# Reordering the first batch of an attention and feed-forward kernel: half of q behind w3, a turn on TensorE, loads without a gate

## The chip, the cores and the metric

The kernel runs on one core of one Trainium2 chip. The metric is the time of one execution on the device in microseconds (us). Three executions of the kernel before gave 397.36, 397.40 and 397.75; the median is 397.4.

The engines of the core work in parallel and meet through semaphores: PE (TensorE, matrix products, with PEld for its weight loads), DVE (VectorE), ACT (ScalarE), POOL (GpSimd, which here mostly issues loads and stores) and SP (SyncE, which here issues the crossbar transposes). PSUM has eight banks, into which PE writes; DVE and ACT read them.

## The reference

A Linformer attention feeds a feed-forward network with a maximum of three products. Batch 8, 8 heads, sequence 1024, head size 64; 64 projected keys; model width 512, inner width 768. All is float32 outside the kernel.

```python
k_proj = einsum('ks,bhsd->bhkd', E, k)
v_proj = einsum('ks,bhsd->bhkd', F, v)
scores = matmul(q, k_proj^T) / sqrt(64)
attn   = softmax(scores)                  # over the 64 projected keys
x      = matmul(attn, v_proj)             # heads side by side: [8192, 512]
h      = maximum(maximum(x @ w1, x @ w2), x @ w3)
out    = h @ w_out                        # [8192, 512]
```

## The kernel before

The kernel works in bfloat16 with sums in float32. The loads convert the type on the way. A batch has two chunks of 512 rows; the feed-forward of a chunk is 18 steps of four 128x512 products (`l1`: six column groups, each with w1, w2 and w3) and four down steps of six products. The attention of the next batch is laid between these steps. The first chunk is special: its weights are still arriving, so it goes through w1, then w2, then w3, and starts on the first half of a weight when that half is there.

The loads at the start, in the order in which POOL issues them (k, v and w1 of the first batch come before):

```python
for wt, w in zip(w_sb[1:], (w2, w3)):
    for hh in range(2):
        if wt is w_sb[2] and hh:
            nc.gpsimd.dma_start(out=q_1, in_=qv_[1])        # q of batch 0, chunk 1
        nc.gpsimd.dma_start(out=wt[:, 2*hh:2*hh+2, :], in_=w[hh*256:(hh+1)*256]...)
...                                                         # cut: work on chunk 0
for x in range(2):
    nc.gpsimd.dma_start(out=wo_sb[:, 3*x:3*x+3], in_=w_out...)
load(1, k, k_t); load(1, v, v_t); load(1, q, q_t)           # batch 1
```

The projection of a batch, its turn, and the gate of the loads after it:

```python
def kv(b, bank=AB):
    for si in range(SI):                                    # eight steps
        nc.tensor.matmul(out=ps[0:KP, bank, :], lhsT=eT[:, si, :], rhs=k_t[i][:, :, si, :], ...)
        nc.tensor.matmul(out=ps[KP:P, bank, :], lhsT=fT[:, si, :], rhs=v_t[i][:, :, si, :], ...)
    nc.scalar.copy(out=kp2[i][:, :, :, 0, :], ...)          # k projected, out of PSUM
    nc.scalar.copy(out=vp2[b % 3][KP:P], ...)
    nc.vector.tensor_copy(out=kp_[:, :, 1:], ...)           # k four times side by side
    nc.vector.tensor_copy(out=vp2[b % 3][0:KP], ...)
    nc.sync.dma_start_transpose(out=kpT[i]..., in_=kp2[i]...)   # the crossbar turns it

def load_behind_turn(b, order="qkv", q_of=None):
    nc.gpsimd.tensor_copy(out=seen, in_=kpT[(b - 1) % NB][:, 0, 0, 0:1])   # the gate
    ...                                                     # cut: load q, k, v of batch b
```

The scores of batch 1 (`scores`, line 143 in the profile) multiply `kpT` with `qT`, which DVE's block transposes (`q_flip`, line 103) make from `q_t`.

The first chunk's steps with w2 and w3, and what lies between them (`tick` counts a slot and starts what `at` has set for it):

```python
def l1_first(i, jts, banks, between=None):
    for hh in range(2):
        if hh and between:
            between()
        for jt, bank in zip(jts, banks):
            for ct in (2 * hh, 2 * hh + 1):
                nc.tensor.matmul(out=ps[:, bank, :], lhsT=w_sb[i][:, ct, ...], rhs=xT[0][:, ct, 0, :], ...)
            if hh:
                nc.vector.tensor_tensor(out=h1c[jt] if i == 1 else hT[0][:, jt, :], ..., op=ALU.max)
                yield

if b == 0:
    at(9, scores_up0)            # scores of batch 0, chunk 1: 64 small products, 4 exponentials
    at(12, sums0, 1, 4)          # their sums: 8 products, logarithm, reciprocal
    at(19, kv, 1)
    ...                          # cut: q_flip at 21, 22, 24, 25; gated loads of batch 2 at 22
    at(27, scores, 1, 0); at(30, scores, 1, 1); at(33, sums, 1)
    ...
for part in ((1, range(6), (6, 7, 0, 1, 4, 5)), (2, range(3), (2, 3, 0), q_up0), (2, range(3, 6), (1, 2, 3))):
    for _ in l1_first(*part):
        tick()
for x in range(2):
    if x:
        av_up0()                 # 16 products with v, 4 divisions on DVE (norm0)
    for tt in range(4):
        down_half(tt, x)         # three products each
        if x: tick()
```

`q_up0` is one DVE block transpose of all of `q_1`. Chunk 1 of batch 0 follows: 18 `l1` steps on slots 17 to 34, and then four down steps.

Of the kernel before, what the change touches and what calls it, by code (L numbers as in the profile page):

```python
# [9 lines left out]
FP32 = mybir.dt.float32  # L10
# [6 lines left out]
def kernel(ctx: ExitStack, tc: tile.TileContext, q, k, v, E, F, w1, w2, w3, w_out, out):  # L17
    nc = tc.nc
    B, H, S, D = q.shape
    KP = E.shape[0]  # L20
# [11 lines left out]
    def T(shape, dt, name):  # L32
        return sb.tile(shape, dt, name=name)

    ps = pp.tile([P, 8, 512], FP32, name="ps")
    psb = ps.rearrange("p b n -> p (b n)").bitcast(BF16).rearrange("p (b n) -> p b n", b=8)

    ident = T([P, P], BF16, "ident")
# [9 lines left out]
    NB = 2  # L48
    k_t = [T([P, H, SI, D], BF16, f"k_t{i}") for i in range(NB)]
    v_t = [T([P, H, SI, D], BF16, f"v_t{i}") for i in range(NB)]  # L50
    q_t = [T([P, H, SI, D], BF16, f"q_t{i}") for i in range(NB)]
    qT = [T([P, H, SI * D], BF16, f"qT{i}") for i in range(NB)]
    kp2 = [T([KP, H, 2, 4, D // 2], BF16, f"kp2_{i}") for i in range(NB)]
    kpT = [T([P, H, 2, KP], BF16, f"kpT{i}") for i in range(NB)]
# [18 lines left out]
    q_1 = q_t[0].rearrange("p h si d -> p (h si d)")[:, 4 * H * D:].rearrange("p (h n d) -> p h n d", h=H, d=D)  # L73
# [41 lines left out]
    AB = 4  # L115
    HD = D // 2

    def kv(b, bank=AB):
        i = b % NB
        for si in range(SI):  # L120
            nc.tensor.matmul(out=ps[0:KP, bank, :], lhsT=eT[:, si, :], rhs=k_t[i][:, :, si, :],  # L121
                             start=(si == 0), stop=(si == SI - 1))
            nc.tensor.matmul(out=ps[KP:P, bank, :], lhsT=fT[:, si, :], rhs=v_t[i][:, :, si, :],  # L123
                             start=(si == 0), stop=(si == SI - 1))
        kp_ = kp2[i].rearrange("k h f r dd -> k (h f) r dd")
        kv_v = ps[KP:P, bank, :].rearrange("p (g u dd f) -> p u g f dd", u=2, f=2, dd=HD)
        nc.scalar.copy(out=kp2[i][:, :, :, 0, :], in_=ps[0:KP, bank, :].rearrange("p (h dd f) -> p h f dd", dd=HD, f=2))  # L127
        nc.scalar.copy(out=vp2[b % 3][KP:P], in_=kv_v[:, 1])
        nc.vector.tensor_copy(out=kp_[:, :, 1:], in_=kp_[:, :, 0:1].to_broadcast([KP, 2 * H, 3, HD]))  # L129
        nc.vector.tensor_copy(out=vp2[b % 3][0:KP], in_=kv_v[:, 0])  # L130
        nc.sync.dma_start_transpose(out=kpT[i].rearrange("p h f k -> p (h f) k"),
                                    in_=kp2[i].rearrange("k h f r dd -> k (h f r dd)"))

    def scores(b, u):
        i = b % NB
# [57 lines left out]
    def fbank():  # L193
        ring.append(ring.pop(0))
        return ring[-1]
# [65 lines left out]
    def quads0(ch, bank, lhs, hhs=(0, 1)):  # L261
        for hh, j, g, u in QUADS:
            if hh not in hhs:
                continue
            rows = half(g, u)
            nc.tensor.matmul(out=ps[j * HD:(j + 1) * HD, bank + hh, :], lhsT=lhs(rows, g),  # L266
                             rhs=pT[0][rows, g, ch, :], start=True, stop=True, tile_position=(rows.start, j * HD))
# [24 lines left out]
    def sums0(ch, bank):  # L292
        quads0(ch, bank, lambda rows, g: ones[rows, :])
        nc.scalar.activation(out=lns[ch], in_=ps[:, bank:bank + 2, :], func=AF.Ln)
        nc.scalar.activation(out=rinv[ch], in_=lns[ch], func=AF.Exp, scale=-1.0)
# [7 lines left out]
    def norm0(ch, half, bank, hhs):  # L303
        for hh in hhs:
            nc.vector.tensor_tensor(out=xT[0][:, 2 * hh + half, ch, :], in0=ps[:, bank + hh, :],
                                    in1=rinv[ch][:, hh * 512:(hh + 1) * 512], op=ALU.mult)
# [9 lines left out]

    qT_1 = qT[0][:, 4:8].rearrange("p a n -> p (a n)").rearrange("p (h n) -> p h n", h=H)

    def q_up0():
        nc.vector.transpose(out=qT_1.bitcast(FP32).rearrange("p h n -> p (h n)"),  # L320
                            in_=q_1.rearrange("p h n d -> p (h n d)").bitcast(FP32))

    def scores_up0():
        for g in range(NPAIR):
# [12 lines left out]
    def av_up0():  # L337
        for f, bank in enumerate((6, 4)):
            quads0(1, bank, lambda rows, g: vp2[0][rows, g, f, :])
        norm0(1, 0, 6, (0, 1))  # L340
        norm0(1, 1, 4, (0, 1))

    def warmup(n, bank):
        for _ in range(n):
# [7 lines left out]
    qv_ = q[0].rearrange("h (ch p n) d -> ch p h n d", ch=2, p=P)  # L352
# [18 lines left out]
    for wt, w in zip(w_sb[1:], (w2, w3)):  # L371
        for hh in range(2):
            if wt is w_sb[2] and hh:
                nc.gpsimd.dma_start(out=q_1, in_=qv_[1])
            nc.gpsimd.dma_start(out=wt[:, 2 * hh:2 * hh + 2, :],
                                in_=w[hh * 256:(hh + 1) * 256].rearrange("(r f) n -> r f n", f=2))
    nc.vector.memset(ones, 1.0)

    for u in range(2):
        for f in range(2):  # L380
            nc.vector.tensor_copy(out=sel[:, 2 * u + f, :].rearrange("p (r dd) -> p r dd", r=4),
                                  in_=ident[:, None, u * D + f:(u + 1) * D:2].to_broadcast([P, 4, HD]))
# [106 lines left out]
    for b in range(B):  # L489
        n = b + 1  # L490
        groups = []

        def at(slot, f, *args):
            groups.append((slot, lambda: f(*args)))

        if b == 0:
            at(9, scores_up0)
            at(12, sums0, 1, 4)
            at(19, kv, 1)
            for g, x in enumerate((21, 22, 24, 25)):  # L500
                at(x, q_flip, 1, g)
            at(22, load_behind_turn, 2, "kvq")
            at(27, scores, 1, 0)
            at(30, scores, 1, 1)
            at(33, sums, 1)
            at(33, log, 1)
            at(34, recip, 0)
            at(35, av3, 1)
            at(36, recip, 1)
            at(36, norm, 1, 1, 0, AB)  # L510
            at(38, norm, 1, 0, 1, AB + 2)
        elif b == 1:
            at(2, kv, 2)
            for g in range(4):
                at(4 + g, q_flip, 2, g)
            at(9, load_behind_turn, 3, "kvq")
            at(9, scores, 2, 0)
            at(12, scores, 2, 1)
            at(16, av1, 1)
            at(16, sums, 2)  # L520
            at(16, log, 1)
            at(17, recip, 0)
            at(19, recip, 1)
            at(24, load, 4, k, k_t)
            at(24, load, 4, v, v_t)
            at(25, av3, 2)
            at(26, norm, 2, 1, 0, AB)
            at(28, norm, 2, 0, 1, AB + 2)
            at(30, kv, 3)
            for g in range(4):  # L530
                at(32 + 2 * g, q_flip, 3, g)
        elif n < B:
            if b + 2 < B:
                at(3, lambda: kv(b + 2, fbank()))
            at(3, scores, n, 0)
            at(8, scores, n, 1)
            if b + 3 < B:
                at(11, load_behind_turn, b + 3, "qkv", 4 if b == 2 else None)
            at(14, av1, b)
            at(14, sums, n)  # L540
            at(14, log, 1)
            at(15, recip, 0)
            at(17, recip, 1)
            at(26, av3, n)
            at(27, norm, n, 1, 0, AB)
            at(29, norm, n, 0, 1, AB + 2)
            if b + 2 < B:
                for g in range(4):
                    at(33 + 2 * g, q_flip, b + 2, g)
        else:  # L550
            at(5, av1, b)
        slot = 0
        gi = 0

        def tick():
            nonlocal slot, gi
            slot += 1
            while gi < len(groups) and groups[gi][0] <= slot:
                groups[gi][1]()
                gi += 1  # L560

        for ch in range(2):
            c = 2 * b + ch
            if c == 0:
                for part in ((1, range(6), (6, 7, 0, 1, 4, 5)), (2, range(3), (2, 3, 0), q_up0), (2, range(3, 6), (1, 2, 3))):
                    for _ in l1_first(*part):
                        tick()
                ring[:] = [0, 1, 2, 3]
                for x in range(2):
                    if x:  # L570
                        av_up0()
                    for tt in range(4):
                        down_half(tt, x)
                        if x:
                            tick()
                continue
            for s in range(18):
                l1(b, ch, c, s // 3, s % 3)
                tick()
                if pend and s in (2, 5, 8, 11):  # L580
                    pend.pop(0)()
                    tick()
            pend = [lambda tt=tt, b=b, ch=ch, c=c: down(b, ch, c, tt) for tt in range(4)]
        if b == 0:
            while pend:
                pend.pop(0)()
                tick()
# [32 lines left out]
```

The softmax here doesn't subtract the row's maximum and nothing guards it: scores larger than these inputs give would overflow.

## Time and profile before

| engine or part | busy us or share |
|---|---|
| span of the profiled execution | 395.7 us |
| PE | 383.8 us, 97% |
| DVE | 202.8 us, 51% |
| ACT | 161.8 us, 41% |
| POOL | 66.4 us, 17% |
| POOL's DMA queue, share of 16 engines | 53.1% |
| SP's DMA queue, share of 16 engines | 5.2% |

A page of the profile has, besides busy times, the chain of work that ended last (each piece is followed back to what released it), groups of instructions with what ended the idle time before them, and a timeline. In the timeline a line is a run of like instructions: start and length in us, engine, source line, operation, what is written and read, form and count; a bracket gives the idle time of the engine just before it and what ended it. Matmuls are pipelined, so their recorded lengths overlap. PEldq is the queue of PE's weight loads: its semaphore waits are listed apart. A DMA whose buffer or queue slot is not free holds up POOL, so POOL's idle times tell when earlier transfers landed.

### The profile page before, as it was taken

What the parts mean: (1) busy time and instruction counts of PE and PEld (TensorE: products, weight loads), DVE (VectorE), ACT (ScalarE), POOL (GpSimd) and SP (SyncE); (2) the same over time, 40 slices, a digit from 0 to 9 for tenths busy, and PEclk for the clock granted to TensorE, in tenths of its full rate; (3) what the DMA queues carried; (4) which work ended last, traced back from release to release, by engine and by line L of the source; (5) the groups of instructions that cost most, each with busy time, mean ns of one, the idle gap of its engine ahead of it and who ended that gap; (6) DMA issues with size and microseconds to landing.
All of it is one profiled execution on the core that took longest, in us unless ns stands there. A gap on an engine that the chain in (4) does not pass through costs nothing.

```text
span 395.7 us, 6653 instructions
## 1 busy us (share of the span) xinstructions
PE 383.8 (97%) x2717; PEld 173.4 (44%) x2768; DVE 202.8 (51%) x302; ACT 161.8 (41%) x248; POOL 66.4 (17%) x109
## 2 busy tenths in 40 slices
PE   8999989999999999999999999999999999999996
PEld 4444434444444444444444444444444444444443
DVE  3447475655662476425764347625664356443342
ACT  4413437455326613356224632266234452222221
POOL 7452123062002501050000500000010000000000
PEclk9999999999999999999999999999999999999999
DMA  8999989979963996169711893121011111101023
GB/s 222 206 208 206 206 156 195 242 112 206 206 157 80 170 206 170 42 118 204 180 57 28 152 206 124 53 59 62 15 53 55 53 55 54 55 34 73 0 106 106
DMA packets 41437, 48.39 MB, mean 122 GB/s; under 512 B 9152, under 2 KB 36544, under 8 KB 41408
## 3 DMA queue, kind: packets, MB, share of 16 engines
q0 software_dynamic: 31776, 43.52, 53.1%
q1 hardware_dynamic: 8656, 3.41, 5.2%
q10 hardware_dynamic: 976, 1.05, 0.8%
q8 instruction: 21, 0.34, 0.4%
q14 instruction: 8, 0.07, 0.0%
HBM read 57.15 MB, written 16.78 MB: 187 GB/s over the span
## 4 chain that ended last, share of the span: by engine, by line
PE 88%; DMA 9%; issue 1%; ACT 0%; DVE 0%; POOL 0%; POOLq 0%; DVEq 0%
PE ps L210 57%; PE ps L235 19%; DMA w_sb<-in_moe_w_dram 3%; PE ps L121 3%; PE ps L157 3%; DMA v_t<-in_v_dram 3%; PE ps L143 2%; DMA k_t<-in_k_dram 2%; DMA kpT<-kp 2%; PE ps L248 1%; PE ps L448 1%; PE ps L228 1%; PE ps L123 0%; PE ps L266 0%; DVE hT L217 0%
## 5 line engine op out<-in xcount | busy, mean ns | idle before, releaser
L210 PE MATMUL ps<-xT,w_sb 128*128 128x512 bf16 x1049 | 242.8, 379 | 1.7
L210 PEld LDWEIGHTS <-w_sb 128*128 128x128 bf16 x1080 | 103.6, 98 | 129.9 <-issue 8.4
L215 DVE TENSOR_TENSOR m<-ps,h1s 128x512 f32<-128x512 f32 x90 | 62.1, 690 | 130.8 <-PE ps L210 99.9
L235 PE MATMUL ps<-wo_sb,hT 128*128 128x512 bf16 x335 | 82.3, 379 | 0.5 <-issue 0.2
L213 ACT COPY h1s<-ps 128x512 f32<-128x512 f32 x90 | 52.9, 588 | 68.6 <-PE ps L210 68.2
L237 ACT COPY o_acc<-ps 128x512 f32<-128x512 f32 x58 | 34.0, 586 | 100.9 <-PE ps L235 85.3
L217 DVE TENSOR_TENSOR hT<-ps,m 128x512 bf16<-128x512 f32 x90 | 62.0, 689 | 11.6 <-PE ps L210 3.9
L242 POOL DMA_DIRECT2D out_dram<-o_acc x28 | 15.2, 541 | 262.9 <-ACT o_acc L237 260.4
L235 PEld LDWEIGHTS <-hT 128*128 128x128 bf16 x348 | 33.5, 98 | 41.4 <-issue 1.9
L175 DVE TENSOR_TENSOR xT<-ps,rinv 128x1024 bf16<-128x1024 f32 x28 | 33.5, 1217 | 9.3 <-PE ps L157 7.3
L148 ACT ACTIVATE pT<-ps 128x1024 bf16<-128x1024 f32 x28 | 27.1, 1020 | 7.6 <-PE ps L143 7.3
L103 DVE STREAM_TRANSPOSE qT<-q_t 128x512 f32<-128x512 f32 x28 | 18.6, 689 | 0.0
L89 POOL DMA_DIRECT2D v_t<-in_v_dram x21 | 15.3, 751 | 10.3 <-DMA q_t<-in_q_dram 3.9
L166 ACT ACTIVATE lns<-ps 128x1024 f32<-128x1024 f32 x14 | 13.6, 1020 | 5.5 <-PE ps L157 5.5
L169 ACT ACTIVATE rinv<-lns 128x1024 f32<-128x1024 f32 x14 | 14.8, 1059 | 0.0
L121 PE MATMUL ps<-k_t,eT 128*64 128x512 bf16 x56 | 13.6, 382 | 0.0
L123 PE MATMUL ps<-v_t,fT 128*64 128x512 bf16 x56 | 13.4, 381 | 0.0
L127 ACT CAST kp<-ps 64x512 bf16<-64x512 f32 x7 | 4.0, 578 | 18.8 <-PE ps L123 18.8
L448 PE MATMUL ps<-xT,w_sb 128*128 128x512 bf16 x46 | 10.6, 379 | 1.0 <-DMA w_sb<-in_moe_w_dram 0.8
L89 POOL DMA_DIRECT2D k_t<-in_k_dram x14 | 10.7, 773 | 3.9 <-DMA k_t<-in_k_dram 1.6
L89 POOL DMA_DIRECT2D q_t<-in_q_dram x14 | 10.6, 777 | 2.1 <-DMA wo_sb<-in_moe_w_out_dram 1.1
L129 DVE COPY kp<-kp 64x1536 bf16<-64x1536 bf16 x7 | 3.9, 552 | 13.1 <-ACT kp L127 13.1
(87 smaller groups left out, 162.5 us busy)
## 6 DMA issues: line engine op xcount, KB each, us to landing
out_dram<-o_acc POOLq DMA_DIRECT2D x30, 512.0 KB, 2.9
q_t<-in_q_dram POOLq DMA_DIRECT2D x15, 512.0 KB, 12.1
k_t<-in_k_dram POOLq DMA_DIRECT2D x14, 512.0 KB, 12.4
v_t<-in_v_dram POOLq DMA_DIRECT2D x18, 256.0 KB, 14.7
v_t<-in_v_dram POOLq DMA_DIRECT2D x7, 512.0 KB, 14.4
w_sb<-in_moe_w_dram POOLq DMA_DIRECT2D x4, 384.0 KB, 10.3
k_t<-in_k_dram POOLq DMA_DIRECT2D x4, 256.0 KB, 8.0
w_sb<-in_moe_w_dram POOLq DMA_DIRECT2D x4, 192.0 KB, 10.0
```

The source lines that it names most:

```text
L89: nc.gpsimd.dma_start(out=dst[b % NB][:, slots], in_=sv[:, heads])
L103: nc.vector.transpose(out=qT[b % NB][:, hs].bitcast(FP32).rearrange("p h n -> p (h n)"), in_=q_t[b % NB][:, hs].rearrange("p h si d -> p ( ...
L121: nc.tensor.matmul(out=ps[0:KP, bank, :], lhsT=eT[:, si, :], rhs=k_t[i][:, :, si, :], start=(si == 0), stop=(si == SI - 1))
L148: nc.scalar.activation(out=pT[i][:, 2 * u + gg].rearrange("p ch (t r n) -> p r (ch t) n", t=4, r=4), in_=ps[:, AB:AB + 4, gg * 256:(gg + 1 ...
L175: nc.vector.tensor_tensor(out=xT[b % 2][:, f::2, ch, :], in0=ps[:, bank:bank + 2, :], in1=rinv[ch].rearrange("p (u n) -> p u n", u=2), op= ...
L210: nc.tensor.matmul(out=ps[:, bank, :], lhsT=w_sb[i][:, ct, jt * P:(jt + 1) * P], rhs=xT[b % 2][:, ct, ch, :], start=(ct == 0), stop=(ct == ...
L213: nc.scalar.copy(out=h1s[jt % 2], in_=ps[:, bank, :])
L215: nc.vector.tensor_tensor(out=m12[jt % 2], in0=ps[:, bank, :], in1=h1s[jt % 2], op=ALU.max)
L217: nc.vector.tensor_tensor(out=hT[c % 2][:, jt, :], in0=ps[:, bank, :], in1=m12[jt % 2], op=ALU.max)
L235: nc.tensor.matmul(out=ps[:, bank, :], lhsT=hT[c % 2][:, jt, tt * P:(tt + 1) * P], rhs=wo_sb[:, jt, :], start=(jt == 0), stop=(jt == NJT - 1))
L237: nc.scalar.copy(out=o[:, tt, :], in_=ps[:, bank, :])
L242: nc.gpsimd.dma_start(out=dst[:, tt - 1:tt + 1, :], in_=o[:, tt - 1:tt + 1, :])
```

## The change

The diff rearranges the first batch and touches nothing from batch 1 on. Its aims: let w3's last half arrive before the half of q that is needed later; let the projection of batch 1 start when v is there; take the crossbar, which shares the DMA engines with the loads, out of the way between that projection and the scores; and let batch 2's loads start without waiting for that turn.

```diff
-    def kv(b, bank=AB):
+    def kv(b, bank=AB, crossbar=True):
...
-        nc.sync.dma_start_transpose(...)
+        if crossbar:
+            nc.sync.dma_start_transpose(...)
+
+    def kp_turn(b):
+        i = b % NB
+        for h in range(H):
+            for f in range(2):
+                x = ((h % 4) * 2 + f) * KP
+                nc.tensor.transpose(out=psb[:, AB + h // 4, x:x + KP], identity=ident[0:KP, 0:KP],
+                                    in_=kp2[i][:, h, f].rearrange("k r dd -> k (r dd)"))
+        for j in range(2):
+            (nc.vector.tensor_copy if j else nc.scalar.copy)(
+                out=kpT[i][:, 4 * j:4 * j + 4]..., in_=psb[:, AB + j, 0:8 * KP])
...
-    def q_up0():
+    def q_up0(hs):                       # one half of the heads
...
-        norm0(1, 0, 6, (0, 1))
-        norm0(1, 1, 4, (0, 1))
+        for hh in range(2):
+            norm0(1, 0, 6, (hh,))
+            norm0(1, 1, 4, (hh,))
...
-                nc.gpsimd.dma_start(out=q_1, in_=qv_[1])
+                nc.gpsimd.dma_start(out=q_1[:, 0:4], in_=qv_[1][:, 0:4])
             nc.gpsimd.dma_start(out=wt[:, 2 * hh:2 * hh + 2, :], ...)
+    nc.gpsimd.dma_start(out=q_1[:, 4:8], in_=qv_[1][:, 4:8])
...
         if b == 0:
-            at(9, scores_up0)
-            at(12, sums0, 1, 4)
-            at(19, kv, 1)
-            for g, x in enumerate((21, 22, 24, 25)):
-                at(x, q_flip, 1, g)
-            at(22, load_behind_turn, 2, "kvq")
-            at(27, scores, 1, 0)
-            at(30, scores, 1, 1)
-            at(33, sums, 1)
-            at(33, log, 1)
-            at(34, recip, 0)
+            at(8, q_up0, slice(4, 8))
+            for x in ((k, k_t), (v, v_t), (q, q_t)):
+                at(18, load, 2, *x)
+            at(22, kv, 1, AB, False)
+            at(23, q_flip, 1, 0)
+            at(24, q_flip, 1, 1)
+            at(24, kp_turn, 1)
+            at(26, scores, 1, 0)
+            at(26, q_flip, 1, 2)
+            at(27, q_flip, 1, 3)
+            at(29, scores, 1, 1)
+            at(32, sums, 1)
+            at(32, log, 1)
+            at(33, recip, 0)
+            at(35, recip, 1)
             at(35, av3, 1)
-            at(36, recip, 1)
             at(36, norm, 1, 1, 0, AB)
-            at(38, norm, 1, 0, 1, AB + 2)
+            at(37, norm, 1, 0, 1, AB + 2)
...
-    part 2: l1_first(2, range(3), (2, 3, 0), q_up0); part 3: l1_first(2, range(3, 6), (1, 2, 3))
+    part 2: l1_first(2, range(3), (2, 3, 0), lambda: q_up0(slice(0, 4)))
+    part 3: l1_first(2, range(3, 6), (1, 2, 3), scores_up0)
...
                         down_half(tt, x)
                         if x:
                             tick()
+                        elif tt == 0:
+                            sums0(1, 4)
```

So the scores of batch 0's second chunk move from ahead of part 3 to its middle, and their sums from its end to behind the first half down step. The projection of batch 1 goes from slot 19 to 22; two steps of `l1` lie between it and the 16 turns on TensorE, and two between these and the first scores.

More of the change, by code (lines that the diff above doesn't have):

```diff
@@ L130, in kv @@
         nc.vector.tensor_copy(out=vp2[b % 3][0:KP], in_=kv_v[:, 0])
-        nc.sync.dma_start_transpose(out=kpT[i].rearrange("p h f k -> p (h f) k"),
-                                    in_=kp2[i].rearrange("k h f r dd -> k (h f r dd)"))
+        if crossbar:
+            nc.sync.dma_start_transpose(out=kpT[i].rearrange("p h f k -> p (h f) k"),
+                                        in_=kp2[i].rearrange("k h f r dd -> k (h f r dd)"))
+    def kp_turn(b):
[7 more added lines that the diff above has]
+            (nc.vector.tensor_copy if j else nc.scalar.copy)(
+                out=kpT[i][:, 4 * j:4 * j + 4].rearrange("p h f k -> p (h f k)"), in_=psb[:, AB + j, 0:8 * KP])
     def scores(b, u):
@@ L317 @@
     qT_1 = qT[0][:, 4:8].rearrange("p a n -> p (a n)").rearrange("p (h n) -> p h n", h=H)
-    def q_up0():
-        nc.vector.transpose(out=qT_1.bitcast(FP32).rearrange("p h n -> p (h n)"),
-                            in_=q_1.rearrange("p h n d -> p (h n d)").bitcast(FP32))
+    def q_up0(hs):
+        nc.vector.transpose(out=qT_1[:, hs].bitcast(FP32).rearrange("p h n -> p (h n)"),
+                            in_=q_1[:, hs].rearrange("p h n d -> p (h n d)").bitcast(FP32))
     def scores_up0():
@@ L564 @@
             if c == 0:
-                for part in ((1, range(6), (6, 7, 0, 1, 4, 5)), (2, range(3), (2, 3, 0), q_up0), (2, range(3, 6), (1, 2, 3))):
+                for part in ((1, range(6), (6, 7, 0, 1, 4, 5)), (2, range(3), (2, 3, 0), lambda: q_up0(slice(0, 4))),
+                             (2, range(3, 6), (1, 2, 3), scores_up0)):
                     for _ in l1_first(*part):
```

## The prediction

> **What bounds the kernel now.** I read the page's busy shares first, then the waits of PE, then PE's timeline around each wait, then POOL's timeline to learn when the loads landed.
>
> ```profile
> PE 383.8 (97%) x2717; PEld 173.4 (44%) x2768; DVE 202.8 (51%) x302; ACT 161.8 (41%) x248; POOL 66.4 (17%) x109
> PE 88%; DMA 9%; issue 1%; ACT 0%; DVE 0%; POOL 0%; POOLq 0%; DVEq 0%
> ```
>
> The first line is the busy time of each engine, the second the chain that ended last, by engine. PE is busy for 383.8 of 395.7 us, so at most 11.9 us can come from waits; 3.6 of them lie in the last 9.7 us (PE busy 6.11 from 386 on) and 1.8 in the first 10 (busy 8.18), neither of which the diff touches. DMA has 9% of the chain because everything before 32 us hangs on the weights. What remains for this change is in PE's waits (us in total, times, longest):
>
> ```profile
> PE ps L143 <- DMA kpT<-kp: 1.1, 1, 1.1
> PE ps L448 <- DMA w_sb<-in_moe_w_dram: 0.8, 1, 0.8
> PE ps L439 <- DMA w_sb<-in_moe_w_dram: 0.6, 1, 0.6
> PE ps L157 <- DVE hT L217: 0.5, 1, 0.5
> ```
>
> Two of these four are what the diff aims at. PE's timeline (start, us, instruction; in brackets the idle time before it) places them:
>
> ```profile
> 25.18 6.64 PE L448 MATMUL ps<-xT,w_sb 128*128 128x512 bf16 x29
> 32.56 1.47 PE L448 MATMUL ps<-xT,w_sb 128*128 128x512 bf16 x6 [0.75 <-DMA w_sb<-in_moe_w_dram]
> 33.96 0.76 PE L329 MATMUL ps<-qT,kp 32*64 32x128 bf16 x64
> ...
> 46.23 0.40 PE L121 MATMUL ps<-k_t,eT 128*64 128x512 bf16 x1
> 46.62 0.38 PE L123 MATMUL ps<-v_t,fT 128*64 128x512 bf16 x1
> ...
> 48.43 7.08 PE L210 MATMUL ps<-xT,w_sb 128*128 128x512 bf16 x31
> 56.57 0.66 PE L143 MATMUL ps<-qT,kpT 32*64 32x256 bf16 x32 [1.05 <-DMA kpT<-kp]
> ```
>
> The reader is to see three losses. At 31.8 PE stops for w3's second half. At 56.5 the scores of batch 1 stop for kpT, which the crossbar turns. The third shows no idle time: the first product with v starts at 46.62, 0.39 after the first product with k, where in batch 2 both start at 72.45. The source view of that line says why (min/median/max ns):
>
> ```profile
> L123 PEldq EVENT_SEMAPHORE x2: 51/1265/2479, 44.0 to 44.1; - x2
> ```
>
> A wait of 2479 ns that begins near 44.0 ends at 46.5: v of batch 1 lands just then. The group takes 2.22 us (46.30 to 48.52 in the chain of waits), in batch 2 1.84 (72.52 to 74.36), so 0.38 us are lost here.
>
> POOL's timeline tells when loads landed, because each descriptor issue waits for an earlier transfer:
>
> ```profile
> 31.18 0.71 POOL L89 DMA_DIRECT2D v_t<-in_v_dram  x1 [1.97 <-DMA q_t<-in_q_dram]
> 32.81 0.76 POOL L89 DMA_DIRECT2D q_t<-in_q_dram  x1 [0.91 <-DMA w_sb<-in_moe_w_dram]
> 56.58 0.19 POOL L93 COPY seen<-kpT 128x1 bf16<-128x1 bf16 x1 [11.40 <-DMA kpT<-kp]
> ```
>
> q of batch 0 landed by 31.15, w3's last half at 32.5. The loads of batch 2 stood behind the gate until 56.6; from 56 to 58 the DMA engines moved nothing (0 GB/s in both one-microsecond stretches).
>
> **What the Trainium skill says.** "DMA: Bandwidth & Descriptors", Issuing engines are not separate DMA queues: transfers begun by SP, ACT or POOL run on the same 16 engines and interleave. The trace agrees: the crossbar's turn from SP takes 3.5 us to landing as the median of seven, and 6.8 the time it meets POOL's queue (374 to 398 GB/s of output from 50 to 53 us). "VectorE: DVE Perf Modes", The three transpose paths: 128x128 in bf16 takes 390 ns on TensorE and 1309 by the crossbar, and TensorE's goes to PSUM. "TensorE: Matmul & The Clock Gate", Part 4: PE-mode transpose, adds that PSUM must then be copied out. The trace has TensorE's form for q: 219 ns for one, but 8 in 0.61 us, so (0.61-0.22)/7 = 56 ns apart. "Perfetto Trace Analysis", Identifying the Most-Contended Engine, warns that matmul busy time overstates, because matmuls are pipelined. It holds here: a 128x512 product lasts 379 ns but 12 take 2.59 us in the chain, 0.216 apart. I count PE's work at 0.216, not at 0.379.
>
> **The change part by part.**
>
> *Half of q behind w3.* The q load of 512 KB ahead of w3's last half becomes 256 KB. At 205 GB/s (the one-microsecond stretches from 28 to 35 have 199 to 222) that is 262 KB/205 = 1.28 us, so w3 lands at 32.5-1.28 = 31.2. PE arrives at 31.8. The whole 0.75 goes, with 0.6 us to spare: **-0.75**.
>
> The other half of q lands where w3 landed, near 32.5. VectorE flips it after the second maximum of the group. The first half's flip starts behind the maxima that end at 32.1 and takes 1.23/2, two maxima take 0.62 each, so the second flip starts near 33.9 and ends near 34.55. PE now puts six more products of w3 ahead of the scores: 31.8 + 12x0.216 = 34.4. Only the third of four pairs needs the second half, 0.35 us later, at 34.75. No wait, though 0.2 us of slack is thin. The third bank of those products is freed by the second maximum at 33.9 and wanted at 33.97: also thin.
>
> *Sums behind the first down step.* They need a bank that all four exponentials read, 2.06 us from the end of the scores. Between lie six and three products, 1.94, and the 0.16 that PE loses after those small tiles now also: 2.10. **+0.05**. The division and the down steps behind it keep their distances, so chunk 1 starts 0.7 earlier, at about 43.0 by the chain (43.71 before).
>
> *The projection three steps later.* k and v meet 6 steps of 4x0.216 instead of 3: 43.0+5.2 = 48.2. v landed at 46.5, and the bytes ahead of it are the same. The 0.38 goes: **-0.38**.
>
> *The turn on TensorE.* Kept from batch 2: ScalarE's copy 0.07 after the group, 0.58; VectorE's copies 0.55 and 0.42, all done 1.68 after the group's end (74.36 to 76.04). Two steps of PE lie between, 1.73: no wait. The 16 turns have 128 columns of weights and 64 moving; 128 moving columns cost 56 ns each, so 16x56 = 0.9 at most and half of that if the moving columns set it. I take 0.75, and 0.1 for changing form: **+0.85**. The copies out of PSUM: ScalarE's stands behind one h1s copy; VectorE's behind flip, maximum, flip, three of about 0.62 from 1.68 on, so 3.55, and 0.42 for the copy (as the q turns' copy): 3.97 after the group. Scores come at 1.73+0.85+1.73 = 4.3. No wait; **-1.05** from the crossbar.
>
> *Loads of batch 2 ungated.* They start when output of chunk 0 is through, near 53.3, and not at 57, and end about 4 us earlier. In the kernel before, the projection of batch 2 at 72.45 did not wait for them, so they are worth nothing by themselves. The gate read kpT after the crossbar's turn, to keep the loads from getting ahead of it; without that turn there is nothing to keep clear. Batch 2's own crossbar turn then meets an emptier queue; its scores did not wait either.
>
> *The rest of batch 0* keeps its work; scores, sums and division come one or two steps earlier against the last steps. From batch 1 on the order on PE is the same, so all of it shifts as one block.
>
> Sum: -0.75+0.05-0.38+0.85-1.05 = -1.28. **397.4 - 1.3 = 396.1 us.**
>
> **Rivals.**
>
> 1. *The turn waits for its own chain.* For it: VectorE was busy 4.63 of 5 us between 50 and 55, and the distances above leave 0 to 0.3 us. Against: ScalarE was busy only 1.01 there, and one crossbar wait is exchanged for two copies of half a microsecond. If the copy to kpT slips by one maximum and one flip, scores wait 1 us and only the first two gains remain: 396.9 to 397.2.
> 2. *The front stays bound elsewhere.* If the engines interleave the two halves of q with w3 so that w3 lands at 32 or later, or the second flip holds the scores, 0.3 to 0.6 of the 0.75 comes back: 396.5. For it: q and w3 together took 4.0 us from 28.5 to 32.5, yet w3 came only 1.35 after q, so their packets overlap. Against: 0.6 us of margin.
> 3. *More than counted goes.* The wait of 0.5 at 88.4 (batch 1, PE on hT) might vanish with an emptier DMA queue. Against: its chain is ScalarE's exponentials, an h1s copy and two maxima, all in batch 1's unchanged order. With it: 395.6.
> 4. *The new loads harm someone.* Ungated loads share engines with the output of chunk 1. Nothing on PE waits for output. I give this little.
>
> **Range and chances.** The terms I trust to 0.2 are the front, v and kpT; the turn is good to 0.4; the three runs before span 0.4. Together 395.5 to 396.9. A change of 2% is 8 us; PE's idle time outside the two ends is 11.9-3.6-1.8 = 6.5, so faster by over 2% has 0.005. Slower by over 2% would need a lost overlap in every batch, and only batch 0 is reordered: 0.005. Within 2%: 0.99.
>
> **What would show each step.** Right: no bracket on the line of w3's last six products; both first products of the projection within 0.05 us of each other; a new group of 16 turns lasting 0.5 to 1.1 us with no bracket, and scores of batch 1 without a wait; DMA without the hole at 56 to 58; batch 1's first projection at 71.2 instead of 72.5, and that same 1.3 us at the end. Wrong: a bracket before the turn, before the scores after it, or before the third pair of batch 0's scores; or a shift at the end that differs from the shift at batch 1's projection, which would mean that a later batch changed too.

## The result, and the profile after

The changed kernel takes 396.19 us (median of 6; 395.83 to 396.98), the kernel before in the same rounds 397.47 (median of 6). The ratio is 0.9969, 95% interval 0.9956 to 0.9982: faster by 0.3%, and clear of noise. The prediction was 396.1.

The page of the changed kernel, busy times and the chain that ended last, by engine:

```profile
PE 384.5 (98%) x2733; PEld 173.7 (44%) x2784; DVE 203.3 (52%) x304; ACT 162.7 (41%) x249; POOL 66.9 (17%) x109
PE 92%; DMA 5%; issue 1%; ACT 1%; DVE 0%; POOL 0%; POOLq 0%; DVEq 0%
```

PE has 0.7 us more work (16 more instructions) in a span that is 1.5 shorter. DMA's share of the chain falls from 9 to 5%: the crossbar's turn and the last wait for w3 have left it. The waits of PE (us in total, times, longest) say the same:

```profile
PE ps L453 <- DMA w_sb<-in_moe_w_dram: 0.5, 1, 0.5
PE ps L169 <- DVE hT L229: 0.5, 1, 0.5
```

The two waits that the diff aimed at are gone; the two that it left alone are there (L453 and L169 are the lines 439 and 157 of before; in the same way 462 is 448, 341 is 329, 260 is 248, 278 is 266, 222 is 210, 155 is 143, and 140 is the new turn). PE's timeline:

```profile
25.02 9.41 PE L462 MATMUL ps<-xT,w_sb 128*128 128x512 bf16 x41
34.36 0.76 PE L341 MATMUL ps<-qT,kp 32*64 32x128 bf16 x64
35.28 1.24 PE L462 MATMUL ps<-xT,w_sb 128*128 128x512 bf16 x5 [0.16 <-issue]
36.36 0.81 PE L260 MATMUL ps<-wo_sb,hT 128*128 128x512 bf16 x3
37.28 0.41 PE L278 MATMUL ps<-pT,ones 64*32 64x512 bf16 x8
...
42.82 5.34 PE L222 MATMUL ps<-xT,w_sb 128*128 128x512 bf16 x24
48.10 0.40 PE L121 MATMUL ps<-k_t,eT 128*64 128x512 bf16 x1
48.10 0.40 PE L123 MATMUL ps<-v_t,fT 128*64 128x512 bf16 x1
...
51.78 0.64 PE L140 MATMUL ps<-ident,kp 64*128 64x64 bf16 x16
52.35 1.90 PE L222 MATMUL ps<-xT,w_sb 128*128 128x512 bf16 x8
54.18 0.66 PE L155 MATMUL ps<-qT,kpT 32*64 32x256 bf16 x32
```

The reader is to see one unbroken run of w2 and w3 from 25.02, without the bracket of 0.75 that the first step with w3's last half had; k and v starting together at 48.10; and 16 turns followed by two steps and the scores of batch 1, no bracket anywhere between. The weight queue's wait for v has shrunk to its floor:

```profile
L123 PEldq EVENT_SEMAPHORE  x2: 51/51/51, 45.8 to 45.9; - x2
```

Five marks on PE cut both profiles into the same stages. "Less a step" allows for the one step of `l1` (4x0.216 = 0.86 us) that now lies behind batch 1's first scores instead of ahead of them.

| stage | before | after | difference |
|---|---|---|---|
| start to w2's first product | 25.18 | 25.02 | -0.16 |
| to chunk 1's first product | 18.36 | 17.80 | -0.56 |
| to batch 1's first scores | 13.03 | 11.36 | -1.67, less a step: -0.81 |
| to batch 2's projection | 15.88 | 16.75 | +0.87, less a step: 0.0 |
| to the end of the span | 323.25 | 323.27 | 0.0 |

The first row is not the change: nothing ahead of it differs, and it lies between 24.90 and 25.88 in the profiles of this study. The change is the second and third row, 1.37 us, beside the 1.28 between the medians. Batches 1 to 7 shift as one block.

### The profile page after: what moved, and what is told of

It is laid out like the page before. It is cut to its first block, busy times and chain, and to the rows that moved or that the text cites. A ratio compares the mean times of both kernels' runs of the same rounds, so it can differ in the third digit from the quotient of the medians.

```text
span 394.2 us, 6687 instructions
## 1 busy us (share of the span) xinstructions
PE 384.5 (98%) x2733; PEld 173.7 (44%) x2784; DVE 203.3 (52%) x304; ACT 162.7 (41%) x249; POOL 66.9 (17%) x109
## 3 DMA queue, kind: packets, MB, share of 16 engines
q10 hardware_dynamic: 976, 1.05, 0.8%
## 4 chain that ended last, share of the span: by engine, by line
PE 92%; DMA 5%; issue 1%; ACT 1%; DVE 0%; POOL 0%; POOLq 0%; DVEq 0%
PE ps L222 59%; PE ps L247 19%; PE ps L121 3%; PE ps L169 3%; DMA w_sb<-in_moe_w_dram 3%; PE ps L462 2%; PE ps L155 2%; DMA k_t<-in_k_dram 2%; PE ps L260 1%; PE ps L453 1%; PE ps L240 1%; ACT pT L345 1%; PE ps L278 0%; POOL k_t L373 0%; PE ps L341 0%
## 5 line engine op out<-in xcount | busy, mean ns | idle before, releaser
L89 POOL DMA_DIRECT2D q_t<-in_q_dram x14 | 10.6, 768 | 4.3 <-DMA q_t<-in_q_dram 2.2
L89 POOL DMA_DIRECT2D k_t<-in_k_dram x14 | 10.6, 771 | 3.8 <-ACT o_acc L500 1.4
L462 PE MATMUL ps<-xT,w_sb 128*128 128x512 bf16 x46 | 10.6, 379 | 0.2 <-issue 0.2
```

The source lines that it names most:

```text
L89: nc.gpsimd.dma_start(out=dst[b % NB][:, slots], in_=sv[:, heads])
L462: nc.tensor.matmul(out=ps[:, bank, :], lhsT=w_sb[i][:, ct, jt * P:(jt + 1) * P], rhs=xT[0][:, ct, 0, :], start=(ct == 0), stop=(ct == NCT ...
```

## The experiments

Each kernel below is the changed one with the edit shown, and none leaves out part of the computation. Times are medians in us; the ratio is to the kernel before in the same rounds, with its 95% interval. The kernel before has medians of 397.47 to 397.56 in all rounds; 7 of its 94 executions beside e1 to e11 took 396.2 to 396.5 instead, and why is not known, because no profile caught one. Because the start varies, the last column is the profile's time from w2's first product to the end, which is 370.52 in the kernel before and 369.18 in the changed one.

| kernel | us | ratio | from w2 |
|---|---|---|---|
| changed | 396.19 | 0.9969 (0.9956 to 0.9982) | 369.18 |
| e1 q whole ahead of w3 | 397.16 | 0.9991 (0.9983 to 0.9999) | 369.89 |
| e2 gate back | 396.26 | 0.9972 (0.9962 to 0.9981) | 369.16 |
| e3 crossbar, gated loads | 397.13 | 1.0000 (0.9984 to 1.0016) | 370.30 |
| e4 crossbar, loads ungated | 406.92 | 1.0246 (1.0225 to 1.0267) | 379.77 |
| e5 turn twice | 396.71 | 0.9984 (0.9976 to 0.9991) | 369.55 |
| e6 projection on slot 19 | 397.24 | 0.9991 (0.9983 to 0.9999) | 369.42 |
| e7 sums later | 396.16 | 0.9966 (0.9954 to 0.9978) | 368.99 |
| e8 av1 later | 395.73 | 0.9955 (0.9943 to 0.9968) | 368.66 |
| e9 e7 and e8 | 395.51 | 0.9953 (0.9938 to 0.9968) | 368.49 |
| e10 crossbar in a cleared queue | 397.39 | 0.9999 (0.9991 to 1.0008) | 370.43 |
| e11 e7, e8 and e10 | 396.56 | 0.9986 (0.9976 to 0.9995) | 369.85 |

### e1: the load of q, whole again

```diff
-                nc.gpsimd.dma_start(out=q_1[:, 0:4], in_=qv_[1][:, 0:4])
+                nc.gpsimd.dma_start(out=q_1, in_=qv_[1])
...
-    nc.gpsimd.dma_start(out=q_1[:, 4:8], in_=qv_[1][:, 4:8])
```

> The changed kernel with q's second-chunk load whole again ahead of w3's last half; the order on PE stays as changed. Theory (256 KB more ahead of w3 at 205 GB/s are 1.28 us, of which 0.6 were margin): PE waits 0.7 us before w3's last six products of part 2, and the kernel ends 0.7 us later than the changed one, near 396.9. Rival (the new order on PE or DVE brings the gain at the front, not the load): no wait there, time as the changed one within 0.2.

It is 1.0 slower than the changed kernel by the medians and 0.71 by the profile from w2 on. The wait is back (e1's PE timeline):

```profile
32.51 2.76 PE L461 MATMUL ps<-xT,w_sb 128*128 128x512 bf16 x12 [0.76 <-DMA w_sb<-in_moe_w_dram]
```

So the gain at the front is the 256 KB that no longer lie ahead of w3. The new order on PE alone, which this kernel keeps, brings nothing there. The margin shows in the changed kernel: when w3's last half was issued, how long that load took to land (min/median/max, one load), and POOL's third load of v in batch 1, which waits for it:

```profile
19.73 0.53 POOL L388 DMA_DIRECT2D w_sb<-in_moe_w_dram  x1 [0.58 <-DMA v_t<-in_v_dram]
DMA to landing us min/median/max: 11.3/11.3/11.3
31.59 0.72 POOL L89 DMA_DIRECT2D v_t<-in_v_dram  x1 [1.21 <-DMA w_sb<-in_moe_w_dram]
```

w3 therefore landed at 19.73+11.3 = 31.0 to 31.1, and PE reached it at 25.02+6.63 = 31.65 (6.63 is what the kernel before took from w2's first product to its wait). The slack is 0.6 us, as the prediction had it. POOL's next issue is a late witness: it came 0.5 us after this landing, and 0.3 after that of the kernel before (32.81 and 32.52).

### e2: the gate of batch 2's loads, put back

```diff
-            for x in ((k, k_t), (v, v_t), (q, q_t)):
-                at(18, load, 2, *x)
...
             at(24, kp_turn, 1)
+            at(24, load_behind_turn, 2, "kvq")
```

> The changed kernel with batch 2's loads behind a gate again: a POOL copy that reads kpT after the turn on TensorE. Theory (the earlier loads bring nothing by themselves, batch 2's k and v are needed only at 70.9): within 0.2 us of the changed kernel, the loads start near 53. Rival (the early loads are part of the gain): 0.5 us or more slower, with a wait before batch 2's projection.

Same: 396.26, and 0.02 less from w2 on. The gate opened at 52.79 and the loads followed from 53.32 on (e2's POOL timeline):

```profile
52.79 0.19 POOL L93 COPY seen<-kpT 128x1 bf16<-128x1 bf16 x1 [8.41 <-ACT kpT L143]
```

Taking the gate away is worth nothing by itself. It does bring the loads forward: the last one lands at 69.7 in the changed kernel and at 73.4 with the gate. But nobody waits for them: with the gate the last load of v lands at 67.7, and batch 2's projection needs it at 70.85.

### e3 and e4: the crossbar back, with and without the gate

```diff
-            at(22, kv, 1, AB, False)
+            at(22, kv, 1, AB)
...
-            at(24, kp_turn, 1)
+            at(24, load_behind_turn, 2, "kvq")       # e3 only; there the loads at 18 are left out
```

> The changed kernel with the crossbar's turn in place of TensorE's, and batch 2's loads gated behind it as before. PE saves the 0.68 us of the turn, but must wait for kpT. Theory (the crossbar meets the output of chunk 0, which leaves the queue near 53, and lands at 55 to 56): scores of batch 1 wait 1.4 to 2.5 us, so 0.7 to 1.8 slower than the changed kernel. Rival (3.5 us from issue to landing as the median, so at 54.8, and scores ready at 53.5): wait 1.3, 0.6 slower.

> The crossbar's turn in place of TensorE's, with batch 2's loads ungated as in the changed kernel. Theory (the turn shares the DMA engines with the loads queued before it): kpT lands 7 to 10 us after its issue, scores wait 5 to 8 us, the kernel is 4 to 7 us slower than the changed one: the turn on TensorE is what makes the ungated loads possible. Rival (the crossbar's queue passes the loads): landing within 4 us, 0.6 to 1 slower, as with the gate.

e3 is 0.9 slower than the changed kernel by the medians and 1.12 from w2 on (13 of its 14 times lie between 396.92 and 397.72, one at 401.43). Its profile shows a wait of 1.81 before the scores, from which the 0.68 saved for the turn go off: 1.13. The crossbar landed 4.1 us after its issue, at 55.2, as the theory had it.

```profile
55.26 0.67 PE L155 MATMUL ps<-qT,kpT 32*64 32x256 bf16 x32 [1.81 <-DMA kpT<-kp]
```

e4 is 10.7 slower, more than either theory gave. The landing took 11.6 us, PE stood 9.30, and then its products ran long (e4's PE timeline, and four stretches of its windows: stretch, length, busy time of PE, PEld, DVE, ACT and POOL, granted clock, DMA share and GB/s):

```profile
63.18 1.08 PE L155 MATMUL ps<-qT,kpT 32*64 32x256 bf16 x32 [9.30 <-DMA kpT<-kp]
64.19 4.32 PE L222 MATMUL ps<-xT,w_sb 128*128 128x512 bf16 x11
68.45 0.66 PE L155 MATMUL ps<-qT,kpT 32*64 32x256 bf16 x32
```

```profile
56.00:57.00 1.00, 0.00 (x0) 0.00 (x0) 0.00 (x0) 0.00 (x0) 0.00 (x0) 1.00 1.20 193
57.00:58.00 1.00, 0.00 (x0) 0.00 (x0) 0.00 (x0) 0.00 (x0) 0.00 (x0) 0.57 1.21 195
66.00:67.00 1.00, 1.00 (x4) 0.33 (x3) 0.81 (x2) 0.27 (x1) 0.00 (x0) 0.50 1.24 206
67.00:68.00 1.00, 0.95 (x4) 0.42 (x4) 0.81 (x2) 0.00 (x0) 0.00 (x0) 0.81 1.24 205
```

PE fell idle at 53.9. Between 57 and 58 its granted clock went to one half (a mean of 0.57 means 0.86 us of that stretch at 0.50), and it stayed there into the stretch from 67 to 68, some four us after the work had come back at 63.18. From 63.18 to 68.45 PE did what took 54.18 to 57.47 in the changed kernel: 5.27 instead of 3.29, so 1.98 of the loss is clock. 9.30+1.98-0.68 = 10.6, as measured from w2 on. The loads and the crossbar's turn cannot share the DMA engines here without this loss. That is what the turn on TensorE, or the gate, prevents.

### e5: the turn twice

```diff
-        for h in range(H):
+        for h in (*range(H), *range(H)):
```

> The changed kernel with each of the 16 turns on TensorE done twice (the second writes the same values to the same place). Theory (the turns lie on PE's path and cost 30 ns each, being set by the 64 moving columns): PE's group of 32 takes 1.05 instead of 0.57, the kernel is 0.5 us slower than the changed one. Rival (56 ns each, as the prediction took as the upper limit): 0.9 slower. Second rival (they fill idle time of PE): same time.

0.5 slower by the medians, 0.4 from w2 on. PE's timeline of e5:

```profile
51.82 1.10 PE L140 MATMUL ps<-ident,kp 64*128 64x64 bf16 x32
52.85 1.90 PE L222 MATMUL ps<-xT,w_sb 128*128 128x512 bf16 x8
```

The group takes 52.85-51.82 = 1.03, 0.46 more than the 0.57 of sixteen: 29 ns for each turn, fully on the path.

### e6: the projection early again

```diff
+            at(19, kv, 1, AB, False)
-            at(22, kv, 1, AB, False)
```

> The changed kernel with the projection of batch 1 back on slot 19, three steps earlier, and all else as changed. Theory (v of batch 1 lands at 46.5, whatever PE does): PE reaches the first product with v at 45.4 and waits 1.1 us; 1.1 slower than the changed kernel, less the 0.1 to 0.2 that the projection may hide. Rival (v lands earlier, the 0.38 before was a loss of another kind): as the changed kernel within 0.2, and both first products start together.

1.05 slower by the medians. Its profile caught a late start of w2 (first product at 25.88 instead of 25.02), and so only a small part of the wait; why the start was late is not shown, as the edit touches nothing ahead of it:

```profile
46.37 0.40 PE L121 MATMUL ps<-k_t,eT 128*64 128x512 bf16 x1
46.66 0.38 PE L123 MATMUL ps<-v_t,fT 128*64 128x512 bf16 x1
```

That makes the point more sharply: the product with k came 0.14 later than in the kernel before (46.23), the one with v at 46.66 after 46.62. v's landing does not follow PE. And the end follows v: from the first product with v to the end of the span it takes 395.3-46.66 = 348.6 us here and 394.2-48.10 = 346.1 in the changed kernel, a difference of 2.5 for the three steps of 0.86 that now lie behind it. So a late start of PE is swallowed by the wait for v, and the loss stands in the medians.

### e7: the sums behind the second half down step

```diff
-                        elif tt == 0:
+                        elif tt == 1:
                             sums0(1, 4)
```

> The changed kernel with batch 0's sums of chunk 1 behind the second half down step instead of the first. Theory (the sums wait 0.2 us for the fourth exponential, though the profile shows no bracket): the step from the scores to chunk 1 of batch 0 shortens by 0.2 us, and with it the kernel. Rival (the spacing of 0.27 is only the change of form on PE): no gain; second rival: the logarithm and the division come too late for chunk 1 and 0.3 is lost.

The medians do not tell it apart from the changed kernel (396.16 and 396.19, with intervals of 0.5 us to either side). The profile does: from w2's first product to chunk 1's first it takes 42.74-25.11 = 17.63 instead of 17.80, and 0.19 less to the end. PE's timeline of e7:

```profile
34.45 0.76 PE L341 MATMUL ps<-qT,kp 32*64 32x128 bf16 x64
35.15 1.47 PE L462 MATMUL ps<-xT,w_sb 128*128 128x512 bf16 x6
36.45 1.46 PE L260 MATMUL ps<-wo_sb,hT 128*128 128x512 bf16 x6
37.84 0.41 PE L278 MATMUL ps<-pT,ones 64*32 64x512 bf16 x8
```

The sums now begin 37.84-36.45-6x0.216 = 0.09 after the down step's work; in the changed kernel it was 37.28-36.36-3x0.216 = 0.27. The 0.18 between is a wait for the exponentials that no bracket shows, because the recorded tail of the products covers it. The chain that ended last names it in the changed kernel (start, us, what):

```profile
35.16 2.07 ACT pT L345 x4
37.28 0.41 PE ps L278 x8
```

This trace settles a second thing. It has all six products behind the scores, and no bracket; the changed kernel's has five of six, and a bracket of 0.16. That bracket is a product missing from the records: from the scores to the first down step it takes the same 2.00 us in both (36.45-34.45 and 36.36-34.36).

### e8: av1 and the sums of batch 1 one slot later

```diff
-            at(16, av1, 1)
-            at(16, sums, 2)
-            at(16, log, 1)
-            at(17, recip, 0)
-            at(19, recip, 1)
+            at(17, av1, 1)
+            at(17, sums, 2)
+            at(17, log, 1)
+            at(18, recip, 0)
+            at(20, recip, 1)
```

> The changed kernel with av1 and the sums of batch 1 one slot later. Theory (the wait of 0.5 us at 87 is for a PSUM bank whose reader on DVE is held up by the exponentials on ACT one slot before): the 0.5 goes, the kernel is 0.5 us faster than the changed one. Rival (the late maxima move along, the wait is found again at the new place): same within 0.2.

The wait of 0.5 is gone and 0.5 us with it, by both measures (395.73; 0.52 less from w2 on). PE's timeline of e8 goes on without a bracket where the changed kernel's stood:

```profile
87.24 0.41 PE L169 MATMUL ps<-pT,vp 64*32 64x512 bf16 x8
```

### e9: both shifts

> The changed kernel with both shifts: batch 0's sums behind the second half down step, and av1 with the sums of batch 1 one slot later. Theory (the two losses are apart and add): 0.2 and 0.5 us, so 0.7 faster than the changed kernel, near 395.5; from w2's first product to the end 368.5 us in the profile (369.2 in the changed kernel's). Rival (only the second was real): 0.5 faster.

395.51 and 368.49 from w2 on, 0.69 less than the changed kernel: the two losses are apart and add. This is the fastest kernel of the study, 0.5% faster than the kernel before. Its PE has no wait left between 24 us and the last batch's end that the profile names.

### e10 and e11: the crossbar in a cleared queue

```diff
-            if tt % 2 == 1:                       # in down_half: the output of chunk 0
-                nc.gpsimd.dma_start(out=out_0[0][:, tt - 1:tt + 1, :], in_=o_acc[0][:, tt - 1:tt + 1, :])
...
-            (loads of batch 2 at 18, kv on 22 and kp_turn on 24)
+            at(21, kv, 1, AB)
+            at(22, load_behind_turn, 2, "kvq")
+            at(22, out_first)                     # the same output, for tt 1 and 3
```

> The changed kernel with the crossbar's turn in place of TensorE's, but in a cleared queue: the projection one slot earlier (21), the output of chunk 0 not sent before the turn but behind batch 2's loads, and these gated behind the turn. Theory (the turn's 6.8 and 11.6 us are waiting behind other transfers, alone it takes 3 to 3.5): kpT lands near 53.5 to 53.9, PE reaches the scores at 53.5, and since PE saves 0.68 us for the turn the kernel is 0.3 to 0.7 faster than the changed one. Rival (the turn is slow by itself with this shape): 1 us or more slower, with a wait before the scores of batch 1.

> All three: the sums later, av1 later, and the crossbar in a cleared queue. Theory: the gains add, 1.0 to 1.4 us faster than the changed kernel, 394.8 to 395.2. Rival (the output and the loads, both moved behind the turn, delay batch 2's own crossbar turn and its scores): a new wait near 78, and no more than the 0.7 of the first two.

Both miss the theory. e10's POOL and PE timelines:

```profile
54.15 0.19 POOL L93 COPY seen<-kpT 128x1 bf16<-128x1 bf16 x1 [18.77 <-DMA kpT<-kp]
```

```profile
54.14 0.66 PE L155 MATMUL ps<-qT,kpT 32*64 32x256 bf16 x32 [0.62 <-ACT h1s L225]
...
80.16 0.66 PE L155 MATMUL ps<-qT,kpT 32*64 32x256 bf16 x32 [1.20 <-DMA kpT<-kp]
```

The crossbar was issued at 50.36 and landed 3.7 us later, at 54.1: quick in a queue cleared of the output, nearly as the theory had it, but 0.2 to 0.6 later than it wanted. (The queue was not empty: q of batch 1 landed at 51.5.) The first bracket names ACT; POOL's gate opens at the same moment on kpT, and e11 has kpT in that place, so kpT it is. Up to these scores e10 is as fast as the changed kernel: 54.14-24.97 = 29.17 us from w2's first product, beside 54.18-25.02 = 29.16. The loss comes later. The second bracket is the transfer put off: batch 2's own crossbar turn was issued at 74.06, when the last of the delayed loads had just landed, and the outputs behind them were still under way until 79.2 (the changed kernel's had landed by 73.7). That turn took 6.1 us. 0.62+1.20-0.68 = +1.14, and 1.25 was measured from w2 on. e11 has the same two waits (0.48 and 1.40), and they more than eat the 0.7 of e9: it ends 0.67 later than the changed kernel from w2 on. Its rival had named the new wait, but not its size.

## Why the prediction was right

The total and its parts, in the order of the prediction. The measured terms are distances on PE's timeline.

| term | predicted | measured | how |
|---|---|---|---|
| w3 half a q load earlier | -0.75 | -0.75 | bracket gone; back at 0.76 in e1 |
| sums behind the first down step | +0.05 | +0.19 | the rest of the front's -0.56; e7 takes 0.17 back |
| projection after v has landed | -0.38 | -0.35 | first product to next step: 1.85 after, 2.20 before |
| turn on TensorE | +0.85 | +0.68 | 16 turns 0.57, about 0.1 for changing form; e5 |
| crossbar's wait | -1.05 | -1.14 | 8.14 between steps and scores before, 8x0.863+0.1 = 7.00 of work |
| loads ungated | 0 | 0 | e2 |
| sum | -1.28 | -1.37 | stages: -0.56-0.81 |

That the sum is so close is in part luck: the sums cost 0.14 more than predicted and the turn 0.17 less, and these two misses cancel.

*Half of q behind w3.* Right in size, cause and margin. The prediction took the bytes ahead of w3 off its landing one for one (1.28 us). w3 landed at 19.88+12.64 = 32.52 before and at about 31.05 after: 1.47 earlier, of which 0.16 is the earlier start of this profile, so 1.3. The second rival did not appear, and its ground was a misreading. It took q's landing from POOL's next issue, at 31.15, and so saw w3 only 1.35 behind q. By their own times from issue to landing q came at 18.58+12.1 = 30.7 and w3 at 32.52, 1.8 later, and the 393 KB of w3's half take 1.9 at 205 GB/s: the two loads landed one behind the other. POOL's idle times give the latest moment at which a transfer can have landed, here 0.3 to 0.5 us too late. The two waits called thin, on the third pair of scores and on a bank, did not appear.

*Sums.* The mis-sized term. The prediction leaned on 0.16 us that PE would lose after the small score products. In traces that hold all records (e5, e7) that gap does not exist; it was a missing record, so the exponentials had 1.94 us and not 2.10, and the sums waited. The loss was small only because the error was.

*Turn.* The cost was guessed between two rates, 56 ns and half of that. The measured 29 ns shows the lower: here the 64 moving columns set the rate, beside 56 ns at 128 columns and 216 at 512. The chain through ACT and DVE fitted: the copies to kpT ended at 52.81 (52.22+0.59) and 53.97 (53.59+0.38), the scores came at 54.18. The first rival, a slip by a flip and a maximum, did not happen, with 0.2 us to spare.

*Crossbar's wait.* Right. One reading beside it is off: the stretches from 50 to 53 moved 368 to 398 GB/s, not 374 to 398, and not all of it was output, as q of batch 1 was landing until 51.6.

*Loads ungated.* Right: nothing, and the fourth rival, harm by the new loads, did not appear (e2). Only their end was mis-sized: 69.7 after 76.7 before, so 7 us earlier and not 4. e4 adds what the prediction did not size: with the crossbar in place, ungated loads would have cost 10.7 us, 2.0 of them by PE's clock.

*The third rival*, the wait of 0.5 in batch 1, stayed as argued: it came at the same distance from batch 2's projection. e8 shows that a slot's shift removes it, so it belongs to batch 1's own order and not to the DMA queue.

## What to carry to other kernels

When one engine is busy 97% of the time, write down its gaps and hidden waits one by one, price each from the trace, and subtract the work that the cure adds to that engine: here the sum came within 0.1 us, and each term within 0.2. For when a transfer landed, take its own time to landing or the engine that waited for it, not the next issue in the queue. Moving a small turn from a shared DMA queue onto the bound engine pays if the turn's work (0.68 us) is less than the queue's wait (1.14), and the engine's unbracketed losses, such as two products that should start together and don't, belong in the sum as much as the bracketed ones. A transfer that is put off to clear a queue comes back at the next user of that queue (e10), so look one turn ahead.

## What the runs showed of the hardware that was not expected

- In e4 PE's granted clock halved about 3.2 us after PE had fallen idle (idle from 53.9, mean 0.57 from 57 to 58) and came back some 4 us after work had resumed (63.2, mean 0.81 from 67 to 68). A wait of 9.3 us therefore cost 11.3. In e3 a wait of 1.81 us left the clock at 1.00.
- The crossbar's turn of batch 1's 64x2048 tile took 3.7, 4.1, 6.8 and 11.6 us from issue to landing. What POOL's queue still had to land when it was issued: the last 1.2 us of a load (e10), the last 0.3 us of a load and the output of chunk 0 (e3), the last 1.9 us of a load and that output (the kernel before), the output and 3 MB of loads (e4). Why e3 and the kernel before differ by 2.7 us is not shown beyond that.
- A bracket of 0.16 us after a change of form on PE, released by "issue", goes with one product too few in the count that follows it (5 of 6, 11 of 12). It is a gap in the records and not in the work.
